# Incoming products of the experts as seven products of halves, outputs summed per 256 hidden columns, and a leaky rectifier in one instruction

## The chip, the cores and the metric

The kernel runs on one core of a Trainium2 chip. A core has TensorE (PE, matrix products into the PSUM banks), VectorE (DVE), ScalarE (ACT), GpSimd (POOL) and SyncE (SP, which issues the transfers). The metric is the device time of one execution in microseconds (us), the median of several.

## The reference

Three steps follow one another. An mLSTM over 2 x 8 heads, 768 positions and head size 40 gives x with 1536 tokens x 320. A dense layer makes g = max(0.01 h, h) with h = x @ w_in (320 x 2048, in 64-bit floats here) and x2 = g @ w_out. Then a mixture of 8 experts, all of them computed for all tokens:

```python
logits = x @ w_gate; logits = logits - logits.max(); P = np.exp(logits)
for _ in range(8):
    P /= P.sum(1, keepdims=True) + 1e-09
    P /= P.sum(0, keepdims=True) + 1e-09
    P *= N / E
for e in range(E):                        # E = 8, w1[e] 320 x 1024, w2[e] 1024 x 320
    h = np.maximum(x @ w1[e], 0.0)
    out += P[:, e:e + 1] * (h @ w2[e])
```

## The kernel before

Every wide product is made of fp32r products: an operand is split into a rounded part ("hi", written by ACT) and the rest ("lo", a subtraction on DVE or POOL), and hi\*hi, hi\*lo and lo\*hi are added up in PSUM. A depth of 320 rows is three row blocks, the third with 64 rows; its hi and lo share one block, so `mm1` (L144) needs eight matmuls for one output tile. `mm2` (L151) is the second layer: three matmuls of 320 columns for 128 tokens and 128 hidden columns.

The first stage (to about 299 us) does the gates, the attention by chunks of 128 positions (`Chunk`) and the dense layer in 96 steps of 128 hidden columns x 256 tokens (`up` L408, `down` L421). In a step ACT makes 0.01 h (L413), DVE the maximum (L414), ACT its hi part (L417), POOL its lo part (L418). Between the steps DVE unpacks the 64-bit weights (L124 to L132). `turn2` transposes the finished x2 into `x2T` (three blocks of 512 tokens) and splits it. This stage is put in order by a planner, by the order of the program and by when it thinks things are ready; the lists `before[g]` and `after[g]` give the order.

The expert stage is in the order in which it is written (`manual_schedule`, L571): each engine takes its instructions strictly one after the other. A group g is one expert, 512 tokens and 128 hidden columns: `up_c` (L651) issues eight matmuls of 512 columns into one PSUM bank, ACT takes hi of the rectified bank (L657), DVE lo (L658); `down_c` (L662), two groups behind, adds 4 x 3 matmuls of 320 columns into four banks `yc`, which are kept for the eight groups of an expert's 1024 columns and only then weighted into `acc` on DVE (L676; for expert 0 copied, L674). There are 8 x 3 x 8 = 192 groups. Beside them: the weights of the next expert, loaded by SP and split on ACT and POOL (L136, L137), and in the first 16 groups or so the gate: `logits`, its transposes, and eight rounds of `rows` (L627, four small DVE instructions) and `columns` (L633, a matmul and four DVE instructions). When the gate is done POOL scales the first expert's outputs (L683).

Of the kernel before, what the change touches and what calls it, by code (L numbers as in the profile page):

```python
# [37 lines left out]
def mlstm_moe_kernel(ctx, tc, qp, q3, kp, kn, vn, gates_in, og, cst_in, scr_in, w_in, w_out, w_gate, w1, w2, out):  # L38
# [23 lines left out]
    xp = ctx.enter_context(tc.tile_pool(name="xp", bufs=2))  # L62
# [23 lines left out]
    class Unit:  # L86


        def __init__(self, w1_ap, w2_ap, nm, is64=False):
            self.src, self.nm, self.is64 = (w1_ap, w2_ap), nm, is64  # L90
            self.t, self.raw, self.up = [None, None], [None, None], [None, None]
# [64 lines left out]

    def transpose_x(ps_pool, x, dst, nm):
# [14 lines left out]
    unitsE = {}  # L172
    x2T, xs2 = {}, {}

    def turn2(j, pool, part=None):
        jb = j * BA // NTC
        if jb not in x2T:
            x2T[jb] = x2p.tile([P, 5, NTC], F32R, tag=f"x2T{jb}", name=f"x2T{jb}")
        for t in (0, 1) if part is None else (part,):
            tok = j * BA + t * P  # L180
            transpose_x(pool, xs2[j][t], x2T[jb][:, :, tok % NTC:tok % NTC + P], f"b{j}_{t}")

    with ExitStack() as st1:
        ac = st1.enter_context(tc.tile_pool(name="ac", bufs=1))
        ap = st1.enter_context(tc.tile_pool(name="ap", bufs=1))
        ha = st1.enter_context(tc.tile_pool(name="ha", bufs=5))
# [81 lines left out]
        kw = ap.tile([P, 9, D], F32, tag="kw", name="kw")  # L268
# [4 lines left out]
        class Chunk:  # L273
# [58 lines left out]
            def weigh(self):  # L332
                self.Pm = self.place([P, 8, P], "Pm", "w1u")
# [38 lines left out]
            def carry(self):  # L372
# [7 lines left out]
                else:  # L380
                    dm = ap.tile([P, G, GV], F32, tag="dm", name=f"dm_{self.nm}")
# [15 lines left out]
        unitsA = [Unit(w_in[i], w_out[i], f"a{i}", wide) for i in range(NUA)]  # L397
        unitsE[0] = [Unit(w1[0, i], w2[0, i], f"e0_{i}") for i in range(NUE)]
# [9 lines left out]
        def up(g):  # L408
# [4 lines left out]
            nc.scalar.activation(gg, h_ps, AF.Copy, scale=0.01)  # L413
            nc.vector.tensor_tensor(gg, h_ps, gg, op=ALU.max)  # L414
# [6 lines left out]
        def down(g):  # L421
# [9 lines left out]
            if f == NFA - 1:  # L431
                xs2[j] = []
                for t in range(2):
                    y = yp[j][t]
                    xs = xp.tile([P, DM], F32, tag="xs", name=f"xs2_{j}_{t}")
# [4 lines left out]
                    xs2[j].append(xs)  # L440
# [27 lines left out]
        before[NFA + HALF + LAG + 0].insert(0, lambda: turn2(1, ps_b))  # L468
        for j in [0] + list(range(2, NBA - 1)):
            before[max(j + 1, 2) * NFA + LAG + 1].insert(0, lambda j=j: turn2(j, ps_b))  # L470
# [28 lines left out]
        for n in range(2 * NUE):  # L499
            i, p = n // 2, n % 2  # L500
            after[g5 - 3 + n].append(lambda i=i, p=p: unitsE[0][i].load(p))
            after[g5 + LAG + 7 + p].append(lambda i=i, p=p: run(unitsE[0][i].convert(p, nc.vector)))
# [16 lines left out]
        zero = ap.tile([P, G * GV], F32, tag="dm", name="zero").bitcast(BF16)  # L519
# [52 lines left out]
    hc = ctx.enter_context(tc.tile_pool(name="hc", bufs=4))  # L572
    cp = ctx.enter_context(tc.tile_pool(name="cp", bufs=1))
    ps_s = ctx.enter_context(tc.tile_pool(name="ps_s", bufs=1, space=PSUM))
    ps_y2 = ctx.enter_context(tc.tile_pool(name="ps_y2", bufs=1, space=PSUM))

    ones = cp.tile([P, P], F32, tag="ones", name="ones")
    nc.gpsimd.memset(ones, 1.0)
    acc = [cp.tile([P, DM], F32, tag=f"acc{t}", name=f"acc{t}") for t in range(NCK)]
    Pg = cp.tile([P, NCK, E], F32, tag="Pg", name="Pg")  # L580

    wgr = cp.tile([P, 3, E], F32, tag="wgr", name="wgr")
    nc.sync.dma_start(wgr, w_gate)
    wg = cp.tile([P, 3, 2, E], F32R, tag="wg", name="wg")
# [240 lines left out]
```

## Time and profile before

| | us |
|---|---|
| Three runs | 1000.46, 1000.84, 1002.84 (median 1000.84) |
| Profiled execution, its own time | 1002.96 |
| Its span | 1001.2 |
| PE busy in the span | 977.7 (98%) |
| DVE, ACT, POOL busy | 378.2, 302.6, 241.6 |
| First and last matmul start of `hc` (expert stage) | 298.9 and 991.9 |

The span is the time from the first to the last instruction; the execution's own time is a little longer. A busy PE is a PE that has work, not one that works at its peak: matmuls overlap in the records, so their pace is read from the distance of their starts. The granted clock of TensorE is given in tenths or as a share: 1.00 is 2.4 GHz, 0.50 is 1.2 GHz.

### The profile page before, as it was taken

To read this page: it belongs to the slowest core of one execution; us is meant where nothing else is said; L and a number is where in the kernel's file an instruction comes from. 1 tells how busy PE (TensorE), PEld (TensorE's weight loads), DVE (VectorE), ACT (ScalarE), POOL (GpSimd) and SP (SyncE) were. 2 spreads that over 40 slices of the span, in tenths; PEclk is the share of its full clock that TensorE was granted. 3 is DMA by queue.
4 is the path that set the end of the run, shared out by engine and by line. 5 is a ranking of instruction groups with operands and counts; after the bars stand their busy time and mean duration, and the time that the engine had idled before them with its cause. 6 is when DMAs were issued, how large, how long until landed. Compare 5 with 4: busy or idle time off the path is not lost.

```text
span 1001.2 us, 14301 instructions
## 1 busy us (share of the span) xinstructions
PE 977.7 (98%) x5917; PEld 886.3 (89%) x5917; DVE 378.2 (38%) x745; ACT 302.6 (30%) x570; POOL 241.6 (24%) x211
## 2 busy tenths in 40 slices
PE   8599999999999999999999999999999999999998
PEld 4488899999998889999999999999999999999997
DVE  5969945343442365222222221222222222222222
ACT  4636444534552221222122122212212212221111
POOL 3454644443430120621012021102202201210000
PEclk8569999999999999999999999999999999999999
DMA  8533503111030110011011011001201100100000
GB/s 264 190 133 108 166 23 105 29 51 38 15 101 16 45 43 16 29 47 42 1 58 44 16 29 59 29 14 45 59 1 43 45 29 14 59 1 1 27 27 27
DMA packets 23526, 52.25 MB, mean 52 GB/s; under 512 B 2614, under 2 KB 9958, under 8 KB 23462
## 3 DMA queue, kind: packets, MB, share of 16 engines
q1 hardware_dynamic: 23462, 51.35, 16.6%
q8 instruction: 46, 0.75, 0.3%
q14 instruction: 18, 0.15, 0.0%
HBM read 49.37 MB, written 1.97 MB: 51 GB/s over the span
## 4 chain that ended last, share of the span: by engine, by line
PE 90%; DVE 6%; DMA 2%; issue 1%; ACT 1%; POOL 1%; SPq 0%; DVEq 0%; POOLq 0%; ACTq 0%
PE hc L146 35%; PE yc L153 11%; PE yc L155 11%; PE yc L154 11%; PE ha L146 8%; PE ya L153 2%; PE ya L154 2%; PE ya L155 2%; PE yps L343 2%; DMA raw_a<-in_w_in_dram 1%; PE sps L329 1%; DVE raw_a L128 1%; PE zps L347 1%; DVE raw_a L132 1%; PE aps L319 1%
## 5 line engine op out<-in xcount | busy, mean ns | idle before, releaser
L146 PE MATMUL hc<-x2T,w1u_e 128*128 128x512 f32 x1536 | 384.0, 392 | 0.0
L146 PEld LDWEIGHTS hc<-x2T,w1u_e 128*128 128x128 f32 x1536 | 280.6, 188 | 49.6
L658 DVE SCALAR_TENSOR_TENSOR hl<-hc,hh 128x512 fp32r<-128x512 f32 x192 | 132.8, 692 | 496.5 <-ACT hh L657 496.5
L657 ACT ACTIVATE hh<-hc 128x512 fp32r<-128x512 f32 x192 | 115.0, 599 | 535.0 <-PE hc L146 531.7
L153 PE MATMUL yc<-w2u_e,hh 128*128 128x320 f32 x768 | 237.5, 309 | 0.6 <-DVE acc L674 0.6
L155 PE MATMUL yc<-w2u_e,hl 128*128 128x320 f32 x768 | 237.3, 309 | 0.0
L154 PE MATMUL yc<-w2u_e,hh 128*128 128x320 f32 x768 | 237.0, 309 | 0.0
L153 PEld LDWEIGHTS yc<-w2u_e,hh 128*128 128x128 f32 x768 | 144.2, 188 | 8.3 <-issue 1.0
L154 PEld LDWEIGHTS yc<-w2u_e,hh 128*128 128x128 f32 x768 | 144.2, 188 | 6.9
L155 PEld LDWEIGHTS yc<-w2u_e,hl 128*128 128x128 f32 x768 | 144.2, 188 | 0.0
L137 POOL TENSOR_TENSOR w1u_e<-raw_e,w1u_e 128x768 fp32r<-128x768 f32 x28 | 51.7, 1847 | 315.5 <-ACT w1u_e L136 315.5
L146 PE MATMUL ha<-xT,w1u_a 128*128 128x256 f32 x768 | 113.3, 292 | 9.8 <-DVE xT L167 3.3
L146 PEld LDWEIGHTS ha<-xT,w1u_a 128*128 128x128 f32 x768 | 104.1, 196 | 15.7 <-ACT xT L165 4.0
L418 POOL TENSOR_TENSOR hla<-gg,hha 128x256 fp32r<-128x256 f32 x90 | 73.9, 822 | 110.4 <-ACT hha L417 93.4
L137 POOL TENSOR_TENSOR w2u_e<-raw_e,w2u_e 128x640 fp32r<-128x640 f32 x28 | 43.9, 1568 | 145.9 <-ACT w2u_e L136 145.9
L414 DVE TENSOR_TENSOR gg<-ha,gg 128x256 f32<-128x256 f32 x96 | 40.3, 421 | 69.4 <-ACT gg L413 69.1
L153 PE MATMUL ya<-w2u_a,hha 128*128 128x320 f32 x192 | 62.8, 327 | 0.0
L154 PE MATMUL ya<-w2u_a,hha 128*128 128x320 f32 x192 | 60.8, 317 | 0.0
L155 PE MATMUL ya<-w2u_a,hla 128*128 128x320 f32 x192 | 60.7, 316 | 0.0
L413 ACT ACTIVATE gg<-ha 128x256 f32<-128x256 f32 x96 | 36.7, 382 | 73.2 <-PE ha L146 73.2
L417 ACT ACTIVATE hha<-gg 128x256 fp32r<-128x256 f32 x96 | 39.9, 416 | 46.0 <-DVE gg L414 45.8
L676 DVE SCALAR_TENSOR_TENSOR acc<-yc,Pg,acc 128x320 f32<-128x320 f32 x84 | 40.3, 543 | 2.6 <-PE yc L155 2.6
(138 smaller groups left out, 695.7 us busy)
## 6 DMA issues: line engine op xcount, KB each, us to landing
raw_e<-in_w_dram SPq DMA_DIRECT2D x32, 384.0 KB, 3.1
raw_e<-in_w_dram SPq DMA_DIRECT2D x32, 320.0 KB, 2.9
raw_a<-in_w_in_dram SPq DMA_DIRECT2D x8, 768.0 KB, 5.2
raw_a<-in_w_out_dram SPq DMA_DIRECT2D x8, 640.0 KB, 3.9
kP_c<-in_kp_dram SPq DMA_DIRECT2D x11, 256.0 KB, 3.1
qP_c<-in_qp_dram SPq DMA_DIRECT2D x11, 256.0 KB, 3.8
vt_c<-in_vn_dram SPq DMA_DIRECT2D x11, 184.5 KB, 2.5
sig<-in_og_dram SPq DMA_DIRECT2D x3, 640.0 KB, 7.3
```

The costliest lines, as they stand in the source:

```text
L137: (lo or nc.gpsimd).tensor_tensor(t[:, n:2 * n], src, t[:, 0:n].bitcast(F32), op=ALU.subtract)
L146: nc.tensor.matmul(h_ps, t1[:, ws, c * P:(c + 1) * P], xt[:, xs, t0:t0 + n], start=(j == 0), stop=(j == len(MM1) - 1),)
L153: nc.tensor.matmul(y_ps, a, t2[:, c, :], start=first, stop=False)
L154: nc.tensor.matmul(y_ps, a, t2[:, 2 + c, :], start=False, stop=False)
L155: nc.tensor.matmul(y_ps, b, t2[:, c, :], start=False, stop=last)
L413: nc.scalar.activation(gg, h_ps, AF.Copy, scale=0.01)
L414: nc.vector.tensor_tensor(gg, h_ps, gg, op=ALU.max)
L417: nc.scalar.activation(hh, gg, AF.Copy)
L418: (nc.vector if g in V_STEPS else nc.gpsimd).tensor_tensor(hl, gg, hh.bitcast(F32), op=ALU.subtract)
L657: nc.scalar.activation(hh, h_ps, AF.Relu)
L658: nc.vector.scalar_tensor_tensor(out=hl, in0=h_ps, scalar=0.0, in1=hh.bitcast(F32), op0=ALU.max, op1=ALU.subtract)
L676: nc.vector.scalar_tensor_tensor(out=acc[tt], in0=yc[t], scalar=Pg[:, tt, e:e + 1], in1=acc[tt], op0=ALU.mult, op1=ALU.add)
```

## The change

**Expert stage.** The work is now cut into 32 units of 256 hidden columns (`Products`, four to an expert) times two halves of 768 tokens: 64 steps. Depth (2 x 160), hidden columns (2 x 128) and tokens (2 x 384) are each halved, and the 2 x 2 x 2 product is made with seven products in place of eight: each takes a sum or difference of weight blocks (`sums`) and one of token blocks (`Position.sums`). A half depth of 160 is a block of 128 rows and one of 32; of the latter the three terms (hi, lo) lie in one block of 96 rows. So one product is three matmuls with 128 rows and one with 96, all of 384 columns: 28 per step. Partial products stay in four banks; DVE adds them up from PSUM and SBUF (`u2`, `u3` and three `c`), ACT rectifies each `c` twice (rounded and full), POOL takes the difference; the fourth output is still made as before. `down_c` now ends after 256 hidden columns: six token blocks, 2 x 3 matmuls each, through three rotating banks, and each is added to `acc` on DVE: six DVE instructions per step. `Position` turns and splits x2: three positions of the first half at the end of the first stage, three of the second half in the first steps of the expert stage. Work beside the matmuls is hung at slots (step, slot): slots 0 to 6 follow the seven products of the next step, 7 to 12 the six token blocks.

**First stage.** One ACT instruction with the function Prelu replaces the scaled copy and the maximum. `turn2` is gone. The small tiles of the attention lie as views in the room that later holds the split x2.

**Gate.** The logits read the new blocks (30 matmuls of 384 columns in place of 15 of 512); a round is spread over seven slots.

```diff
-            nc.scalar.activation(gg, h_ps, AF.Copy, scale=0.01)
-            nc.vector.tensor_tensor(gg, h_ps, gg, op=ALU.max)
+            nc.scalar.activation(gg, h_ps, AF.Prelu, alpha=0.01)
...
+        def load1(self):                          # class Products
+            for h in range(2):
+                nc.sync.dma_start(dst[:, h, :, 0], src[:, h])
+                for r in range(4):
+                    nc.sync.dma_start(dst[r * KM:(r + 1) * KM, h, :, 1], src[h * KM:(h + 1) * KM, 2])
+        def sums(self, eng, part=None):
+            for k, (o, x, y, op) in enumerate(((4, 1, 3, ALU.add), (1, 0, 1, ALU.subtract), (5, 4, 0, ALU.subtract),
+                                               (6, 2, 5, ALU.subtract))):
+                if part is None or k in part:
+                    eng.tensor_tensor(r[:, o], r[:, x], r[:, y], op=op)
+        def split1(self, k, lo, rest):
+            split7(self.raw[:, (0, 4)[k]:(4, 7)[k]], self.w1[k], slice(0, P), KM, lo, rest)
+        def split2(self, lo):
+            nc.scalar.activation(t[:, 0:2], self.raw2, AF.Copy)
+            lo.tensor_tensor(t[:, 2:4], self.raw2, t[:, 0:2].bitcast(F32), op=ALU.subtract)
+    def split7(raw, dst, t, r0, lo, rest):
+        nc.scalar.activation(dst[:, :, 0:2, t], raw.rearrange("p n (s t) -> p n s t", s=2), AF.Copy)
+        lo.tensor_tensor(dst[:, :, 2, t], raw[:, :, 0:P], dst[:, :, 0, t].bitcast(F32), op=ALU.subtract)
+        r = slice(r0, r0 + KM)
+        rest.tensor_tensor(dst[r, :, 1, t], raw[r, :, P:2 * P], dst[r, :, 1, t].bitcast(F32), op=ALU.subtract)
+        def turn(self, k, pool, copy):            # class Position, k = 0 or 1
+            if k == 0:
+                for i, x in enumerate((xa, xb)):
+                    copy(self.rr[:, i]..., x[:, 2 * P:DM]...)
+            for j, (i, x, h) in enumerate(((0, xa, 0), (0, xa, 1), (1, xb, 1), (1, xb, 0))):
+                nc.tensor.transpose(pt[:, j, :], self.rr[:, i, h] if k else x[:, h * P:(h + 1) * P], ident)
+            nc.scalar.activation(self.raw[:, 0:4, k * P:(k + 1) * P], pt, AF.Copy)
+        def sums(self, eng):
+            for o, x, y in ((5, 2, 3), (3, 3, 0), (4, 2, 3), (6, 1, 4)):
+                eng.tensor_tensor(r[:, o], r[:, x], r[:, y], op=ALU.subtract)
...
+        for g, fn in ((g5 - 6, experts[0].load1), (g5 + 1, lambda: prepare_position(positions[0][0])),
+                      (g5 + 5, lambda: prepare_expert(experts[0])), (g5 + 6, experts[0].load2),
+                      (g5 + 6, lambda: prepare_position(positions[0][1])), (g5 + 7, experts[1].load1),
+                      (g5 + 10, lambda: prepare_position(positions[0][2])),
+                      (g5 + 11, lambda: experts[0].split2(nc.gpsimd)), (g5 + 11, experts[1].load2),
+                      (g5 + 13, lambda: prepare_expert(experts[1])), (g5 + 14, experts[2].load1)):
+            after[g].append(fn)
...
+    def product(bank, u, q, w, x, fresh):
+        f, b = u.factor(w), X[q][:, x]
+        nc.tensor.matmul(bank, f[:, 0], b[:, 0], start=fresh, stop=False, skip_group_check=not fresh)
+        nc.tensor.matmul(bank, f[:, 0], b[:, 2], start=False, stop=False, skip_group_check=not fresh)
+        nc.tensor.matmul(bank, f[:, 2], b[:, 0], start=False, stop=False, skip_group_check=not fresh)
+        nc.tensor.matmul(bank, f[0:K3, 1], b[0:K3, 1], start=False, stop=True, skip_group_check=not fresh)
+    def up_c(i):
+        def out_of(a, b, part, plus):
+            nc.vector.tensor_tensor(c, part, plus, op=ALU.add)
+            nc.scalar.activation(hh[a][b], c, AF.Relu)
+            nc.scalar.activation(c, c, AF.Relu)
+            nc.gpsimd.tensor_tensor(hl[a][b], c, hh[a][b].bitcast(F32), op=ALU.subtract)
+        product(bank[0], u, q, 0, 0, True)
+        nc.scalar.activation(p1, bank[0], AF.Copy)
+        product(bank[1], u, q, 5, 4, True)
+        nc.vector.tensor_tensor(u2, bank[1], p1, op=ALU.add)
+        product(bank[2], u, q, 1, 5, True)
+        nc.vector.tensor_tensor(u3, bank[2], u2, op=ALU.add)
+        product(bank[3], u, q, 4, 3, True)
+        out_of(1, 1, bank[3], u3)
+        product(bank[0], u, q, 2, 1, False)
+        nc.scalar.activation(hh[0][0], bank[0], AF.Relu)
+        nc.vector.scalar_tensor_tensor(out=hl[0][0], in0=bank[0], scalar=0.0, in1=hh[0][0].bitcast(F32), ...)
+        product(bank[2], u, q, 3, 6, False)
+        out_of(1, 0, bank[2], u2)
+        product(bank[3], u, q, 6, 2, False)
+        out_of(0, 1, bank[3], u2)
...
+    for p, (t0, t1, g, s) in enumerate((((-1, 0), (-1, 3), -1, 5), ((-1, 6), (0, 2), 0, 3), ((0, 5), (0, 8), 0, 9))):
+        hook(*t0, turn_x1(p, 0))
+        hook(*t1, turn_x1(p, 1))
+        hook(g, s, lambda p=p: fill_x1(p))        # sums on DVE, split on ACT, DVE and POOL
+    at0, PERIOD = 2 * 13 + 7, 7                   # rows and columns: a round every 7 slots
+            hook(7 + q, (0, 0, 1, 1, 2, 2)[t], lambda q=q, t=t: scale_first(q, t))
+    hook(-1, 2, lambda: experts[2].sums(nc.vector))
+    for n in range(3, NU):
+        u, g = experts[n], max(2 * n - 4, 3)
+        hook(g - 2, 0, u.load1)
+        for k in range(4):
+            hook(g, 8 + k, lambda u=u, k=k: u.sums(nc.gpsimd, (k,)))
+        hook(g + 1, 8, lambda u=u: u.split1(0, nc.gpsimd, nc.gpsimd))
+        hook(g + 1, 10, lambda u=u: u.split1(1, nc.gpsimd, nc.gpsimd))
+        hook(g + 1, 12, u.load2)
+        hook(g + 2, 8, lambda u=u: u.split2(nc.gpsimd))
```

## Rows read from the trace of the kernel before

**Rows 1.** Stages: stretch, its length, PE, PEld, DVE, ACT, POOL busy (instructions), clock, DMA.

```profile
70.00:125.00 55.00, 51.49 (x389) 47.27 (x389) 51.51 (x100) 29.84 (x66) 28.70 (x25) 1.00 0.44 139
125.00:268.00 143.00, 142.89 (x1142) 137.88 (x1141) 62.93 (x165) 63.95 (x150) 59.62 (x76) 1.00 0.15 43
268.00:298.80 30.80, 30.48 (x232) 30.21 (x232) 14.69 (x29) 18.60 (x44) 13.44 (x17) 1.00 0.26 75
298.80:405.00 106.20, 105.61 (x594) 93.05 (x594) 46.46 (x113) 25.84 (x44) 15.80 (x10) 1.00 0.11 34
405.00:997.70 592.70, 592.59 (x3303) 537.26 (x3302) 151.63 (x249) 130.86 (x212) 92.61 (x58) 1.00 0.10 30
```

**Rows 2.** Timeline of one group of the expert stage: start, length, instructions.

```profile
602.24 2.00 PE L146 MATMUL hc<-x2T,w1u_e 128*128 128x512 f32 x8
604.08 0.30 PE L153 MATMUL yc<-w2u_e,hh 128*128 128x320 f32 x1
...
605.83 2.00 PE L146 MATMUL hc<-x2T,w1u_e 128*128 128x512 f32 x8
```

**Rows 3.** Groups of instructions, whole span: count, busy us, mean ns, idle before.

```profile
L658 DVE SCALAR_TENSOR_TENSOR hl<-hc,hh 128x512 fp32r<-128x512 f32 x192 | 132.8, 692 | 496.5 <-ACT hh L657 496.5
L676 DVE SCALAR_TENSOR_TENSOR acc<-yc,Pg,acc 128x320 f32<-128x320 f32 x84 | 40.3, 543 | 2.6 <-PE yc L155 2.6
L414 DVE TENSOR_TENSOR gg<-ha,gg 128x256 f32<-128x256 f32 x96 | 40.3, 421 | 69.4 <-ACT gg L413 69.1
L417 ACT ACTIVATE hha<-gg 128x256 fp32r<-128x256 f32 x96 | 39.9, 416 | 46.0 <-DVE gg L414 45.8
L137 POOL TENSOR_TENSOR w1u_e<-raw_e,w1u_e 128x768 fp32r<-128x768 f32 x28 | 51.7, 1847 | 315.5 <-ACT w1u_e L136 315.5
L137 POOL TENSOR_TENSOR w2u_e<-raw_e,w2u_e 128x640 fp32r<-128x640 f32 x28 | 43.9, 1568 | 145.9 <-ACT w2u_e L136 145.9
```

**Rows 4.** The same view, shapes kept apart.

```profile
L136 ACT ACTIVATE w1u_e<-raw_e 128x768 fp32r<-128x768 f32 x32 | 26.8, 838 | 0.9 <-DMA raw_e<-in_w_dram 0.9
L683 POOL TENSOR_SCALAR acc<-acc,Pg 128x320 f32<-128x320 f32 x12 | 12.8, 1087 | 27.0 <-DVE Pg L631 24.2 <-DVE Pg L639 2.8
L137 DVE TENSOR_TENSOR w1u_e<-raw_e,w1u_e 128x768 fp32r<-128x768 f32 x4 | 3.8, 959 | 3.2 <-ACT w1u_e L136 3.2
L211 ACT ACT_TABLE_LOAD x2 | 2.6, 1283 | 0.0
```

**Rows 5.** Timeline of DVE and POOL in two stretches of the expert stage.

```profile
351.40 0.25 DVE L636 TENSOR_REDUCE cs<-cps 128x8 f32<-128x96 f32 x1
351.68 1.76 DVE L637 TENSOR_SCALAR cs<-cs 128x8 f32<-128x8 f32 x1
353.72 0.26 DVE L639 SCALAR_TENSOR_TENSOR Pg<-Pg,cs 128x96 f32<-128x96 f32 x1
382.10 0.17 DVE L637 TENSOR_SCALAR cs<-cs 128x8 f32<-128x8 f32 x1
...
351.57 1.85 POOL L137 TENSOR_TENSOR w1u_e<-raw_e,w1u_e 128x768 fp32r<-128x768 f32 x1 [5.09 <-ACT w1u_e L136]
...
598.50 1.85 POOL L137 TENSOR_TENSOR w1u_e<-raw_e,w1u_e 128x768 fp32r<-128x768 f32 x1 [5.73 <-ACT w1u_e L136]
599.70 0.55 DVE L676 SCALAR_TENSOR_TENSOR acc<-yc,Pg,acc 128x320 f32<-128x320 f32 x1
```

**Rows 6.** Timeline of PE around matmuls with fewer than 128 rows, and a transpose.

```profile
236.03 0.27 PE L164 MATMUL pt_b<-cst,xs 128*64 128x128 f32 x1
236.14 0.38 PE L162 MATMUL pt_b<-cst,xs 128*128 128x128 f32 x2
...
239.14 0.31 PE L155 MATMUL ya<-w2u_a,hla 128*128 128x320 f32 x1
239.38 0.72 PE L319 MATMUL aps<-bd,stt 32*128 32x512 f32 x2
240.04 1.22 PE L146 MATMUL ha<-xT,w1u_a 128*128 128x256 f32 x8
...
242.80 0.91 PE L347 MATMUL zps<-Cst,q 120*128 120x123 f32 x6
```

More of the change, by code (lines that the diff above doesn't have):

```diff
@@ L171, in mlstm_moe_kernel @@
     NBA = NT // BA
[L172 to L181, printed above, removed]
+    x2s, X = {}, {}
+    R0 = x2p.tile([P, 21 * NQ], F32, tag="R0", name="R0")
+    experts = [Products(w1[e, i], w2[e, i], f"e{e}_{i}") for e in range(E) for i in range(NUE)]
+    positions = [[Position(q, p) for p in range(HP)] for q in range(2)]
     with ExitStack() as st1:
@@ L396, in mlstm_moe_kernel @@
         NG = NBA * NFA
-        unitsA = [Unit(w_in[i], w_out[i], f"a{i}", wide) for i in range(NUA)]
-        unitsE[0] = [Unit(w1[0, i], w2[0, i], f"e0_{i}") for i in range(NUE)]
+        unitsA = [Unit(i, w_in[i], w_out[i], f"a{i}", wide) for i in range(NUA)]
         chunks = [Chunk(c) for c in range(NCK)]
@@ new lines, in mlstm_moe_kernel, with down_c @@
+    ny = [0]
+    def down_c(i):
+        n, q = order[i]
+        u = experts[n]
+        e = n // NUE
+        hh, hl = hidden.pop(i)
+        if q not in acc:
+            acc[q] = x2p.tile([P, 2 * HP, DM], F32, tag="XT", name="acc1")
+        for b in range(2):
+            for p in range(HP):
+                t = b * HP + p
+                k = ny[0] % 3
+                ny[0] += 1
+                y = (ps_y, ps_y, ps_y2)[k].tile([P, DM], F32, tag=("ya0", "ya1", "yb0")[k], name=f"y{i}_{t}")
+                for a in range(2):
+                    mm2(y, hh[a][b], hl[a][b], p, u.w2, a, a == 0, a == 1)
+                o = acc[q][:, t]
+                if n == 0:
+                    nc.vector.tensor_copy(o, y)
+                elif e == 0:
+                    nc.vector.tensor_tensor(o, y, o, op=ALU.add)
@@ L682, in scale_first @@
-    def scale_first(t):
-        nc.gpsimd.tensor_scalar(out=acc[t], in0=acc[t], scalar1=Pg[:, t, 0:1], scalar2=None, op0=ALU.mult)
-    before = {g: [] for g in range(NGC + LAGC)}
-    after = {g: [] for g in range(NGC + LAGC)}
-    for i in range(2):
-        before[(1, 3)[i]].append(lambda i=i: turn2(NBA - 1, ps_s, i))
-    for j in range(NB):
-        before[(5, 4, 8)[j]].append(lambda j=j: logits(j))
-    G0 = 9
-    before[G0].append(logits_turn)
-    before[G0 + 1].append(top_turn)
-    before[G0 + 2].append(top_all)
@@ L695, in mlstm_moe_kernel @@
-    for it in range(8):
-        after[G0 + 2 + 2 * it].append(rows)
-        before[G0 + 4 + 2 * it].append(lambda it=it: columns(it))
-    for t in range(NCK):
-        after[NS + LAGC + t // 2].append(lambda t=t: scale_first(t))
-    for e in range(1, E):
-        for n in range(2 * NUE):
-            i, p = n // 2, n % 2
-            g = (e - 1) * NS + LAGC + 2 * n
-            after[g].append(lambda e=e, i=i, p=p: units[e][i].load(p))
-            after[g + 3].append(lambda e=e, i=i, p=p: run(units[e][i].convert(p)))
@@ L706, in mlstm_moe_kernel, with scale_first, copy_rest @@
-    for g in range(NGC + LAGC):
-        if g < NGC:
-            up_c(g)
-        for fn in before[g]:
-            fn()
-        if g >= LAGC:
-            down_c(g - LAGC)
-        for fn in after[g]:
-            fn()
+                    nc.sync.dma_start(out[row:row + P, :], o)
+                at(i, 7 + t)
+    def scale_first(q, t):
+        o = acc[q][:, t]
+        nc.gpsimd.tensor_scalar(out=o, in0=o, scalar1=Pg[:, 2 * HP * q + t, 0:1], scalar2=None, op0=ALU.mult)
+    def copy_rest(o, i):
+        nc.gpsimd.tensor_copy(o, i)
@@ L718 @@
+    up_c(0)
+    for i in range(len(order)):
+        if i + 1 < len(order):
+            up_c(i + 1)
+        down_c(i)
+    assert not hooks
 _OUTS = [((1536, 320), 'float32')]
```

247 lines of the change are left out of this document (164 added, 83 removed).

## Prediction

> **What bounds the kernel now.** I read the busy time by stage first [rows 1]. The expert stage takes 298.8 to 997.7, 698.9 us; PE is busy for all of it, DVE for a quarter of 405 to 997.7 and POOL for a sixth. From 125 to 298.8 PE is the bound too. Only 70 to 125 has another: DVE 51.5 of 55 us. The timeline gives PE's pace [rows 2]: a group begins at 602.24, its 320-column matmuls at 604.08, the next group at 605.83. So a 512-column matmul costs 1.84/8 = 0.230 us, a 320-column one 1.75/12 = 0.146, a group 3.59, and 192 groups 689.3 of the 698.9; 9.6 are the gate and transposes. The span of 1001.2 lies 1.8 under the profiled execution's 1002.96, and that lies 2.1 above the median of 1000.84. I work on 1002.96 and take off 2.1 at the end.
>
> **The change, part by part.**
>
> *Matmuls of the experts.* A 384-column matmul lies between the two: 0.146 + 64/192 x 0.084 = 0.174. A step has 28 of them, 4.87 us, and 36 of 320 columns, 5.26: 10.13. The same work is now three groups, 10.77. Saved: 0.64 x 64 = **41.0 us**. In proportion to columns 384 costs 0.1725 to 0.175, so 38 to 44 us. A weight load is hidden already beside 320 columns.
>
> *Matmuls with 96 rows.* A quarter of the 28. The trace has 32 and 120 rows [rows 6]. With 32 rows: 0.24 from the matmul before (0.146 expected), 0.72 - 0.39 = 0.33 from the first to the second of 512 columns (0.230 expected; 0.39 is one's recorded length, 2.00 - 7 x 0.230), 0.33 to the next; some 0.09 lost on entry and 0.09 on exit. With 120 rows six take 0.91, 0.11 to 0.13 apart, what the 128-column transposes take too (236.03 to 236.14): no loss. Bounds 0 and 448 x 0.185 = +83 us; I take 0, since 96 is nearer to 120 and, like it, doesn't fit in half of the rows. The Trainium skill (TensorEngine Tiling, Key Properties) says that a change of the tiling mode drains TensorE, and lists modes of 128, 64 and 32 rows. The 32-row matmuls agree; by that list 96 rows run in the 128-row mode and cost nothing, and the sum would be mine. No run so far shows 96.
>
> *Other PE work.* In the expert stage 30 logits matmuls at 0.174 (5.2) for 15 at 0.230 (3.45), 24 transposes at 0.11 for 8: **+3.5**. In the first stage 40 transposes go and 24 come: **-1.8**.
>
> *A step's other engines.* DVE: six operations of 384 columns, 0.557 each (between 421 ns for 256 and 692 for 512), and six additions into `acc` at 0.543: 6.6 of 10.13. ACT: eight of about 0.5, and of the weights per two steps 1.05 + 0.84 + 0.73: 5.3. POOL costs 2.18 ns a column (1847 to 1568 ns over 128 columns): 0.73 for 256, 1.01 for 384, 1.29 for 512; per two steps 6 x 1.01 + 4 x 0.73 + 2 x 1.29 + 2 x 1.01 + 1.57 = 15.2 of 20.3 [rows 3, 4]. None is over. The tightest wait inside a step: product 3 ends 2.95 us after the step's start (16 x 0.174 and 0.16 by which a record outlasts its pace); DVE's `c` 3.51, two rectifiers of 0.52 4.55, the fourth output's hi on ACT 5.05, its lo on DVE 5.61, two more `c` 6.72, the first `acc` addition 7.27. Its bank is wanted again by the fourth token block at 4.87 + 3 x 0.876 = 7.50. It holds, by 0.23: **0**; bounds 0 and +32 (0.5 a step).
>
> *Filling the second half's blocks* (steps -1 and 0). Each of three `fill_x1` puts on DVE four subtractions (0.42 each) and a low part of 896 columns (959 ns for 768: 1.09), and between them DVE waits for ACT's copy of 1792 columns (0.82 ns a column: 1.7). Behind that waiting subtraction stand the last `c` of the step and the next `u2`, `u3`; product 3 and 5 of the next step wait for their banks, and all PE behind them. So a fill takes DVE 4.5 us, three 13.4, expert 2's `sums` 1.7, the steps' own work (12 x 0.557 and 6 copies) 9.6: 24.7 us where PE has 2 x 4.87 + 5.26 + 2.6 = 17.6. That is 7.1 over. Further, DVE and POOL get in each other's way: an 8-element DVE instruction took 1.76 us and ended with POOL's subtraction, which had begun 0.1 before it; alone it takes 0.17. An `acc` addition, which reads PSUM, took its 0.55 beside POOL [rows 5]. All fill operations are of SBUF alone, 19 of them with `sums`, and POOL has some 22 us of work in this stretch (six low parts 6.1, splits of units 1 and 2 6.2, three rests of 896 columns 6.4, six copies some 3.6): 0.25 each, 5 more. **+12**; bounds 0 (later steps wait less) and +18.
>
> *The gate's rounds* fall on 7 slots of 13, 1.86 rounds a step, over 4.3 steps. A round is two series of DVE instructions of about 1.0 us unhindered (351.40 to 353.98 less the 1.6 waited), so 3.7 a step: with 6.3 it just fits in 10.13. POOL is busy 75% of the time with operations of 1 us, so each of four SBUF instructions in a round waits 0.38: 12 us in eight rounds, part of it in time where DVE would be idle. `columns` stands in PE's queue four slots behind `rows`, so a late DVE stops PE. **+7**; bounds 0 and +20.
>
> *Units 3 and scaling.* Unit 3 is split during `down_c(4)` and wanted directly after it: POOL ends its four subtractions 13.7 us after that step's start, the matmuls want them from 10.6: about 2.5, part of it covered by the waits above. `scale_first` puts 12 x 1.087 us on POOL in two steps where it has 15.2 of 20.3 to do [rows 4]. Together **+3**; bounds 0 and +6.
>
> *First stage.* 21 of the 96 maxima lie in 70 to 125, 21 x 0.42 = 8.8 us of DVE's 51.5. Half of it moves PE: **-4**; bounds -9 and 0. At its end (268 to 298.8) DVE gets three positions (3.9 each) and two experts (2.95 each), 17.5, and loses maxima, x2T and the old splits, 14.8. ACT gets 15.7 and loses 7.3: 27 of 30.8 busy, in bursts of 3.7 us in front of the rectifiers that free two banks. X[0] must be whole before the first product. **+4**; bounds 0 and +12. Prelu itself takes what the scaled copy took. If it isn't in the table that holds Exp, every chunk's Exp adds two loads of 1.283 us [rows 4], 20 of them 26 us of ACT, of which half is idle: 0 to +13; I take 0, since the copies beside Exp load nothing. The Trainium skill (ScalarE: Activation LUTs, Table sets) says that cheap functions lie in every set and names relu, copy, identity and abs; the leaky one is not named. By it the sum would be mine or 13 more; the five loads of the trace agree with it for the named ones.
>
> *Transfers.* Ten for a unit's first weights in place of one, all on SP, issued two steps (20 us) ahead; the DMA engines are 10% busy [rows 1] and nothing but loads and the last outputs stands in that queue. 0.
>
> Sum: -41.0 + 3.5 - 1.8 + 12 + 7 + 3 - 4 + 4 = -17.3; 1002.96 - 17.3 = 985.7, and less 2.1: **983.5 us**.
>
> **The rivals.**
> *Clean start.* The waits of the first steps vanish, because DVE's delays fall into the down phases, where PE needs nothing of it for 5 us: 1000.84 - 41 + 1.7 - 4 = 957.5. For it: four of the terms are overlaps that I added up one by one. Against: three fills stand within 1.5 steps.
> *Narrow matmuls drain PE* (the other side). Each of 448 matmuls of 96 rows costs 0.185 as with 32 rows: 983.5 + 83 - 12 (the waits of the first steps are then covered) = 1055. It decides from 17.3/448 = 0.039 us each. For it: the 32-row rows. Against: the 120-row one.
> *The chain in a step is late.* The 0.23 us of slack are gone and each step waits 0.4: 983.5 + 25.6 = 1009; it decides from 0.27 a step. For it: five hand-overs between ACT and DVE, each some hundredths, are not in my chain. Against: instructions of one engine that follow each other overlap somewhat in the records.
> *The product count doesn't become time*: PE's pace set by weight loads, 28 for 24. Against: 128-column transposes follow at 0.11, under 0.174. Under 1 in 50.
>
> **How the numbers follow.** Forecast 983.5, own range 967 to 999 (the bounds of the first steps' terms): 0.57. Clean start, 950 to 966: 0.17. Chain late, 1000 to 1020: 0.11. Narrow matmuls, 1040 to 1066: 0.07. The rest, 0.08, is Prelu's loads and a first stage put in another order by the planner, 990 to 1010. The range 957 to 1010 leaves out the lower half of the clean start, the narrow matmuls and the late end of the chain, 2 in 10. A change under 0.3% (3 us) can't be told from none. Faster: 0.57 + 0.17 + 0.03 = 0.77; same 0.06; slower 0.17.
>
> **What would show it.** Distance of 384-column matmul starts 0.174, also into and out of 96 rows; a steady step of 10.1 us; waits of PE for DVE in the first 60 us of the expert stage that add up to about 20, and next to none later; the first `product` at about 297 to 300; no more table loads than five. Wrong would make it: steady steps over 10.4 us, DVE's `acc` additions longer than 0.55, POOL over 16 us per two steps, or first steps without waits.

## The result, and the profile after

The changed kernel takes 1008.11 us (median of five, 1007.07 to 1010.63), the kernel before 1000.82 in the same runs (999.90 to 1002.84): ratio 1.0073, 95% interval 1.0054 to 1.0092. It is **slower**, by 0.7%: little, but the interval lies wholly above 1. The forecast was 983.5. The profiled execution took 1007.07, its span 1005.4.

The stages of the kernel after (columns as in [rows 1]):

```profile
70.00:125.00 55.00, 51.93 (x404) 48.68 (x404) 41.84 (x74) 29.00 (x66) 26.40 (x25) 1.00 0.37 114
125.00:268.00 143.00, 142.01 (x1126) 136.93 (x1124) 37.65 (x97) 64.77 (x151) 61.16 (x76) 1.00 0.15 46
297.90:360.00 62.10, 46.33 (x261) 41.36 (x260) 31.35 (x61) 27.27 (x48) 28.94 (x27) 0.86 0.12 32
360.00:455.00 95.00, 82.84 (x493) 79.96 (x492) 64.87 (x155) 37.40 (x71) 62.42 (x63) 0.96 0.09 26
455.00:1001.70 546.70, 546.70 (x3433) 546.39 (x3432) 336.39 (x643) 266.69 (x501) 395.84 (x393) 1.00 0.15 42
```

The first product comes at 297.90, as forecast. Before, PE worked from 298.8 to the end almost without a gap and at a granted clock of 1.00 [rows 1]. Now only the last row looks so. In the two above it PE lacks 28 us of work, and the clock is 0.86 and 0.96. The timeline of a steady step:

```profile
598.41 0.33 PE L777 MATMUL b<-X,w_e 128*128 128x384 f32 x1
...
600.34 0.34 PE L780 MATMUL b<-X,w_e 96*128 96x384 f32 x1
600.51 0.34 PE L777 MATMUL b<-X,w_e 128*128 128x384 f32 x1
...
603.34 0.31 PE L157 MATMUL y<-w_e,hh 128*128 128x320 f32 x1
...
608.62 0.34 PE L777 MATMUL b<-X,w_e 128*128 128x384 f32 x1
```

The step begins at 598.41 and its down phase at 603.34, so 28 matmuls of 384 columns take about 4.9 us and 36 of 320 take 5.28; steps from 455 on take 10.20 us in the mean. Three groups took 10.77 [rows 2]. Into and out of a 96-row matmul the starts are 0.17 to 0.18 apart, as between two of 128 rows. Groups of the kernel after, shapes kept apart:

```profile
L848 DVE SCALAR_TENSOR_TENSOR acc<-y,Pg,acc 128x320 f32<-128x320 f32 x336 | 179.1, 547 | 63.7 <-PE y L159 57.6
L796 DVE TENSOR_TENSOR c<-b,s 128x384 f32<-128x384 f32 x192 | 100.4, 550 | 15.6 <-PE b L780 8.2 <-POOL w_e L205 4.1 <-POOL hl L799 2.4
L232 DVE TENSOR_TENSOR rawx<-rawx 128x256 f32<-128x256 f32 x24 | 16.9, 703 | 4.6 <-ACT rawx L226 4.0
L207 POOL TENSOR_TENSOR X<-rawx,X 32x896 fp32r<-32x896 f32 x3 | 8.8, 2930 | 10.4 <-ACT X L204 10.4
L411 ACT ACT_TABLE_LOAD x2 | 2.6, 1283 | 0.0
```

The additions are as long as assumed (543 and 557). The subtractions of the fills are not: 703 against 421 [rows 3] (675 for the twelve of the second half). There are five table loads (two of them in the last row), as before. What PE waited for from 298 to 455 (us in total, times, longest):

```profile
PE px L225 <- POOL rr L861: 6.4, 1, 6.4
PE px L225 <- ACT w_e L204: 6.0, 1, 6.0
PE y L157 <- DVE acc L846: 5.1, 3, 3.4
PE b L777 <- DVE c L796: 3.6, 3, 1.6
PE b L777 <- DVE s L808: 2.6, 2, 1.5
PE y L157 <- DVE acc L844: 2.4, 1, 2.4
PE cps L747 <- DVE Pg L743: 1.0, 1, 1.0
PE px L225 <- ACT rawx L226: 0.7, 1, 0.7
```

27.8 us in 13 waits: px is the turning of the second half, y the down phases, cps the rounds, b the products. How the 6.0 arises, followed through DVE, ACT, POOL and PE:

```profile
308.99 2.56 DVE L232 TENSOR_TENSOR rawx<-rawx 128x256 f32<-128x256 f32 x4
311.58 1.70 ACT L204 ACTIVATE X<-rawx 128x1792 fp32r<-128x1792 f32 x1 [1.40 <-DVE rawx L232]
313.31 1.09 DVE L205 TENSOR_TENSOR X<-rawx,X 128x896 fp32r<-128x896 f32 x1 [1.76 <-ACT X L204]
313.42 2.92 POOL L207 TENSOR_TENSOR X<-rawx,X 32x896 fp32r<-32x896 f32 x1 [2.15 <-ACT X L204]
314.32 0.55 DVE L796 TENSOR_TENSOR c<-b,s 128x384 f32<-128x384 f32 x1
315.46 0.52 ACT L798 ACTIVATE c<-c 128x384 f32<-128x384 f32 x1
316.42 1.01 POOL L799 TENSOR_TENSOR hl<-c,hh 128x384 fp32r<-128x384 f32 x1
317.36 0.75 POOL L861 COPY rr<-x 128x256 f32<-128x256 f32 x2
317.82 1.11 PE L225 MATMUL px<-cst,rr 128*128 128x128 f32 x4 [5.98 <-ACT w_e L204]
```

The first four rows are fill 0. The last `c` of step 0 stands behind it on DVE, its rectifiers behind that on ACT, `hl` behind those on POOL, the copies of `rr` behind `hl`, and PE's transposes behind `rr`. (POOL has its own part of the fill in front of `hl` too: the rectifier ended at 315.98, that part at 316.34.) So a transpose for the *next* fill, whose blocks are first read at 352.6, stops all matmuls for 6 us. (The profile names ACT's split of unit 2 as the releaser; what ends just before the transpose starts is the first of the two `rr` copies.)

### The profile page after: what moved, and what is told of

Its sections match the earlier page's. It is cut to its first block, busy times and chain, and to the rows that moved or that the text cites. A ratio compares the mean times of both kernels' runs of the same rounds, so it can differ in the third digit from the quotient of the medians.

```text
span 1005.4 us, 16882 instructions
## 1 busy us (share of the span) xinstructions
PE 948.7 (94%) x6188; PEld 918.3 (91%) x6188; DVE 590.6 (59%) x1146; ACT 479.8 (48%) x935; POOL 631.1 (63%) x629
## 4 chain that ended last, share of the span: by engine, by line
PE 74%; DVE 12%; POOL 4%; issue 4%; ACT 3%; DMA 2%; SPq 1%; DVEq 0%; ACTq 0%; POOLq 0%
PE y L157 10%; PE y L158 10%; PE y L159 10%; PE b L777 7%; PE b L780 7%; PE b L779 7%; PE b L778 7%; PE ha L150 6%; PE ya L157 2%; PE ya L159 2%; PE ya L158 2%; PE yps L434 1%; DVE raw_a L132 1%; DVE rawx L232 1%; POOL acc L858 1%
## 5 line engine op out<-in xcount | busy, mean ns | idle before, releaser
L799 POOL TENSOR_TENSOR hl<-c,hh 128x384 fp32r<-128x384 f32 x192 | 196.0, 1023 | 186.5 <-ACT c L798 145.3
L157 PE MATMUL y<-w_e,hh 128*128 128x320 f32 x768 | 239.3, 312 | 7.4 <-DVE acc L846 5.1
L158 PE MATMUL y<-w_e,hh 128*128 128x320 f32 x768 | 238.4, 310 | 0.0
L159 PE MATMUL y<-w_e,hl 128*128 128x320 f32 x768 | 237.9, 310 | 0.0
L848 DVE SCALAR_TENSOR_TENSOR acc<-y,Pg,acc 128x320 f32<-128x320 f32 x336 | 179.1, 547 | 63.7 <-PE y L159 57.6
L777 PE MATMUL b<-X,w_e 128*128 128x384 f32 x448 | 154.7, 345 | 6.3 <-DVE c L796 3.6
L157 PEld LDWEIGHTS y<-w_e,hh 128*128 128x128 f32 x768 | 145.0, 189 | 9.1 <-DVE acc L846 5.9
L780 PE MATMUL b<-X,w_e 96*128 96x384 f32 x448 | 152.5, 340 | 0.0
L779 PE MATMUL b<-X,w_e 128*128 128x384 f32 x448 | 152.2, 340 | 0.0
L778 PE MATMUL b<-X,w_e 128*128 128x384 f32 x448 | 151.8, 339 | 0.0
L158 PEld LDWEIGHTS y<-w_e,hh 128*128 128x128 f32 x768 | 145.1, 189 | 0.0
L159 PEld LDWEIGHTS y<-w_e,hl 128*128 128x128 f32 x768 | 145.1, 189 | 0.0
L150 PE MATMUL ha<-xT,w_a 128*128 128x256 f32 x768 | 112.7, 289 | 10.4 <-ACT gg L503 3.7
L150 PEld LDWEIGHTS ha<-xT,w_a 128*128 128x128 f32 x768 | 102.8, 194 | 16.3 <-ACT gg L503 5.2
L777 PEld LDWEIGHTS b<-X,w_e 128*128 128x128 f32 x448 | 85.9, 192 | 8.5 <-DVE c L796 4.6
L778 PEld LDWEIGHTS b<-X,w_e 128*128 128x128 f32 x448 | 86.1, 192 | 0.0
```

The lines of the kernel that those rows point to most:

```text
L150: nc.tensor.matmul(h_ps, t1[:, ws, c * P:(c + 1) * P], xt[:, xs, t0:t0 + n], start=(j == 0), stop=(j == len(MM1) - 1),)
L157: nc.tensor.matmul(y_ps, a, t2[:, c, :], start=first, stop=False)
L158: nc.tensor.matmul(y_ps, a, t2[:, 2 + c, :], start=False, stop=False)
L159: nc.tensor.matmul(y_ps, b, t2[:, c, :], start=False, stop=last)
L777: nc.tensor.matmul(bank, f[:, 0], b[:, 0], start=fresh, stop=False, skip_group_check=not fresh)
L778: nc.tensor.matmul(bank, f[:, 0], b[:, 2], start=False, stop=False, skip_group_check=not fresh)
```

## The experiments

The first stage is the same code in most of these kernels, yet the first product came between 297.9 and 303.6 in it, with a mean clock of 0.66 to 0.80 in the first 70 us. So beside the times I give the **expert stage** of the profiled execution: end of the span less the start of the first product. It is 702.3 us before and 707.5 after. The same stage came to 707.2 and 708.2 in e9 and e10, so differences of about 1 us say nothing.

**e1: no fills.**

```diff
-    X[1] = cp.tile([P, 7, 3, NQ], F32R, tag="X1", name="X1")
+    X[1] = X[0]                    # and the nine hooks of turn_x1, fill_x1 are gone
```

> Leaves out the turning and filling of the second half's three positions; the second half's products read the blocks of the first half instead. Theory (the fills make PE wait, through DVE and ACT waiting for each other, and PE's clock falls after these waits): the two waits of 6 us for px go, the falls of the clock at 307 to 335 with them; 2.3 us of transposes, some 15 us of waits and some 5 us of cold matmuls: 983 to 988 us, steps -1 to 2 at 11 us each. Rival (the first steps are slow because of the late gate weights, the splits of unit 2 and cold matmuls, whatever is filled): only the transposes and a few us go, 1000 to 1005 us.

989.89 us, just above the theory's range; ratio to before 0.989 [0.983, 0.995]; expert stage 688.1, 19.4 less. The slots of -1 and 0 (the products of steps 0 and 1 and the first down phase) take 21.4 us in place of 40.0; later steps change little. So the fills cost 17.3 us beside their 2.1 us of transposes (six times 0.357).

**e2: no rounds.**

```diff
-    hook(2, 7, rows)
-    for it in range(8): ...        # columns, columns_end, rows
```

> Leaves out the eight rounds that normalise rows and columns (the gate is only the exponential). Theory (the rounds' small DVE instructions, behind POOL's and in front of the acc additions, make PE wait): 1.3 us of matmuls, some 12 us of waits in 355 to 440 and the two falls of the clock at 379 and 396 (3.4) go: 990 to 993 us, steps of 5.0 and 5.3 us there. Rival (POOL is late with the weights of units 3 and 4 in these steps, rounds or not): 1003 to 1006 us, and PE still waits there.

998.11, between the two; ratio 0.996 [0.994, 0.999]; expert stage 697.3, 10.2 less. The steps of the rounds come down to 10.2 us, but step 6, the first with unit 3, takes 12.1 us for its products (4.9 steady). PE's waits from 355 to 455:

```profile
PE b L779 <- POOL w_e L205: 1.8, 1, 1.8
PE b L780 <- POOL w_e L207: 1.5, 2, 0.9
PE b L777 <- DVE c L796: 1.3, 1, 1.3
```

The waits at y are gone. Both were partly right: POOL's split of unit 3 is late, and in the changed kernel, where no wait for it shows, the rounds' waits covered it.

**e3: gate weights loaded early.**

```diff
+        wgr = const.tile(...); nc.gpsimd.memset(wgr, 0.0); nc.sync.dma_start(wgr[...], w_gate[...])   # first stage
```

> The gate weights are cleared and loaded at the start of the first stage; nothing else moves. Theory (DVE stands 7.6 us for them until 302.4, and the first u2, u3 behind it): the first down-phase starts 3 us earlier, 1004 to 1006 us. Rival (the wait is hidden: the first fill's sums and ACT set the pace of these steps anyway): 1007 to 1009 us, the wait for px grows by what is saved.

1011.31, above both; ratio 1.012 [1.006, 1.018]; expert stage 705.9, 1.6 less, hardly more than such stages differ by themselves; the px wait grew from 5.98 to 7.45. The 7.6 us for which DVE had stood were mostly covered by the fill. The profiled execution is longer because the first product came at 303.6. Six transfers more in SP's queue at the start may be why, or the spread of that stage (e7, whose first stage is unchanged, had 303.6 too); neither was tried by itself.

**e4: fills hung apart**, gate and scaling a step later.

```diff
-        positions[1][p].sums(...); positions[1][p].split(...)      # one slot: (-1,5), (0,3), (0,9)
+    sums (0,6) (0,11) (1,7)   ACT's split (0,7) (1,0) (1,8)   low parts (0,9) (1,3) (1,10)
```

> The same instructions of the fills on the same engines, but hung apart: the four subtractions, ACT's split and the low parts each two slots later than what they wait for, most in the down phases of steps 0 and 1 and between the first products of step 2; the second half's logits, the rounds and the scaling a step later. Theory A (queues in strict order: DVE and ACT wait for each other in a fill, with the c's behind them): the two 6 us waits and their cold matmuls shrink, 993 to 999 us. Rival B (what costs is that DVE and POOL work on SBUF at the same time): the same work beside the same work, 1005 to 1010 us, with the DVE sums still at a mean of 700 ns.

1005.39, ratio 1.004 [1.001, 1.007]; expert stage 704.0. The slots of -1 and 0 took 29.0 in place of 40.0, but some five of the 11 us came back in the next two steps (the down phase of step 1 took 9.7 for 7.1), where the last fill met POOL's work (its sums took 1.1 us each in the mean); the mean of all twelve sums rose from 675 to 875 ns. Five more went to step 6, where unit 3 is late again (12.2 us of products for 7.3). A was right on where the waits came from, B on the time and on a part of what replaced them.

**e5: all of it placed anew**, on the same engines. Hooks, as 13 x step + slot:

```
              after                        e5                           e8
sums          -8, 3, 9                     0, 11, 16                    7, 9, 16
ACT's split   the same slots               10, 13, 23                   10, 12, 17
low parts     the same slots               12, 19, 23                   13, 18, 21
columns       37, 44, 51 ... 86            42, 49, 54, 61, 67, 79 ...   43, 47, 53, 62, 71, 80 ...
unit 3        sums 47-50, splits 60, 62    28-36, 40, 53                29-35, 38, 44
gate weights  start of the expert stage    end of the first stage       as e5
```

> Same instructions on the same engines as the changed kernel, all fills, rounds and units kept; only their places among the steps of the expert stage are others (gate weights loaded late in the first stage; rr copies ahead of the low parts; the sums, ACT's split and the low parts of a fill five to ten slots apart; DVE's small instructions of the rounds where POOL has little to do; unit 3 and 4 split steps earlier). Theory (PE's 28 us of waits in 298 to 455 come from DVE, ACT and POOL waiting for each other in strict order, and from DVE and POOL holding each other up on SBUF; 13 us of cold matmuls follow from these waits): all but some 8 us go, the expert stage takes 672 to 682 in place of 707.5, the execution 970 to 983 us, clock 1.0 nearly throughout. Rival (the first 150 us have too much work for DVE and POOL wherever it stands): waits return at other places, 995 to 1006 us.

992.07, ratio 0.990 [0.987, 0.993]: faster than before, and between what theory and rival expected. Expert stage 689.5, 18 less than after, short of the 672 to 682 expected: PE still waited 6.3 us at five `columns` and 5.0 in two waits for `u3`.

**e6: rounds without POOL.**

```diff
+            hook(g + 1, 10, lambda u=u, n=n: setattr(u, "w1", experts[n - 3].w1))     # units 3, 4: no sums, no split
+            if 2 <= i <= 9: nc.scalar.activation(hl[a][b], c, AF.Copy)               # in place of POOL's subtraction
```

> As the changed kernel, but POOL has next to nothing to do in steps 2 to 5, where the rounds stand: the splits of units 3 and 4 are left out (their matmuls read the blocks of units 0 and 1), and in steps 2 to 9 the low part of the three c is a plain copy on ACT. Fills and rounds are unchanged. Theory B (the rounds cost time because their small DVE instructions wait until POOL's instruction ends): PE's waits between 355 and 445 fall from 12 us to under 4, the small instructions keep to 0.17 to 0.27 us each, 994 to 998 us. Rival A (the chain of a round, DVE, PE, DVE, is too long for its seven slots by itself): waits of 9 us or more stay, 1003 to 1008 us.

1004.34, a time of A's range; ratio 1.003 [1.000, 1.006]; expert stage 704.0. The small instructions by line, kernel after first (ns: min/median/max), then e6 (us, mean ns):

```profile
L740 DVE TENSOR_REDUCE rs<-Pg x8: 252/253/254, 362.4 to 416.8; 128x12 f32<-128x96 f32 x8
L742 DVE RECIPROCAL rs<-rs x8: 227/228/229, 363.2 to 417.3; 128x12 f32<-128x12 f32 x8
L741 DVE TENSOR_SCALAR rs<-rs x8: 172/358/1145, 362.7 to 417.1; 128x12 f32<-128x12 f32 x8
L743 DVE TENSOR_TENSOR Pg<-Pg,rs x8: 257/362/1119, 363.5 to 417.6; 128x96 f32<-128x96 f32 x8
L753 DVE SCALAR_TENSOR_TENSOR Pg<-Pg,cs x8: 257/552/1336, 367.6 to 422.8; 128x96 f32<-128x96 f32 x8
```

```profile
L741 DVE TENSOR_SCALAR rs<-rs 128x12 f32<-128x12 f32 x8 | 1.4, 173 | 0.3
L743 DVE TENSOR_TENSOR Pg<-Pg,rs 128x96 f32<-128x96 f32 x8 | 2.1, 258 | 0.3
L753 DVE SCALAR_TENSOR_TENSOR Pg<-Pg,cs 128x96 f32<-128x96 f32 x8 | 2.1, 258 | 0.3
```

With POOL idle these three never stretch; beside it they take up to 6.7 times as long, while the reduction and the reciprocal keep their length. The Trainium skill (SBUF — State Buffer, Who interferes with whom) says that DVE and GpSimd share a port pair under an exclusive lock, which a DVE instruction with two SBUF inputs, or one of the copy and tensor-scalar kind, can take, and that a reduction does not contend. The trace agrees with that; the reciprocal isn't named there. But PE's waits from 355 to 445 fell only from 10.5 to 6.6 us. 2.4 of these follow the exponential, which stands on ACT behind the added copies, and a new wait of 1.8 us for ACT at 351.9 came with the copies too. So both theories hold a part: POOL's meeting with the rounds is worth some 4 to 6 us of waits, and 4 of the 10.5 stay without it.

**e7: no rounds, unit 3 a step earlier.**

```diff
-            hook(g, 8 + k, lambda u=u, k=k: u.sums(nc.gpsimd, (k,)))
+            hook(g - (n == 3), 8 + k, lambda u=u, k=k: u.sums(nc.gpsimd, (k,)))       # the splits likewise
```

> The eight rounds are left out as before, and POOL forms and splits unit 3 one step earlier. Theory (without rounds the step that first uses unit 3 took 12.1 us in place of 4.9, because POOL ends unit 3's blocks only then; with rounds their waits hid it): that step takes 5 us, the expert stage 690 in place of 697, 989 to 993 us. Rival (POOL has too much to do there at any place): the wait moves to another step, 996 to 1000 us.

992.90, ratio 0.991 [0.988, 0.994]; expert stage 689.7, as expected, and the products of step 6 take 4.9. So the rounds and the late unit 3 together cost 17.8 us, 1.2 of them matmuls: 10.2 went with the rounds (e2), 7.6 more with unit 3. No run has the rounds with unit 3 alone moved, so how the 17.8 divide stays open.

**e8: placed once more** (third column of the table; rounds where POOL has little to do, scaling from slot 99 on).

> As the placed version (same instructions, same engines as the changed kernel), with the places chosen once more from what its trace shows: there PE still waits 7 us for the rounds' Pg (five waits of 0.9 to 1.7 us at the columns matmuls), 2.2 us in step 2 and 2.9 us at the scaling. Now each columns matmul stands later behind its rows, units 3 and 4 are split before most rounds, the scaling ends a step earlier. Theory (order and meeting of DVE and POOL): about 10 of the 16 us of waits and 5 of the 10 us of cold matmuls go, the expert stage takes 674 to 682 in place of 689.5, 976 to 986 us. Rival (the rest is work, not place): 988 to 993 us.

982.69, ratio 0.981 [0.978, 0.984]: the fastest of all. Expert stage 681.7. Its waits from 298 to 455, and two stretches:

```profile
PE cps L749 <- DVE Pg L745: 2.9, 4, 0.9
PE y L157 <- DVE acc L846: 1.8, 1, 1.8
PE y L157 <- DVE acc L848: 1.4, 2, 1.3
PE y L157 <- DVE acc L850: 1.3, 2, 0.8
...
```

```profile
298.00:360.00 62.00, 57.33 (x348) 52.31 (x348) 44.19 (x88) 34.63 (x62) 41.61 (x43) 0.97 0.10 28
360.00:455.00 95.00, 90.99 (x564) 88.89 (x564) 63.02 (x156) 41.50 (x78) 70.97 (x70) 1.00 0.13 37
```

8.6 us of waits in place of 27.8, and with them went the low clock: 0.97 and 1.00 for 0.86 and 0.96. The fill's subtractions still meet POOL, and are longer than in the changed kernel (822 ns for 675), but nothing that PE wants soon stands behind them.

**e9: the changed kernel again**, on the chip that ran e8.

> The changed kernel itself, unchanged, so that the placed versions are compared with it on one chip: 1004 to 1010 us, expert stage 706 to 709 us.

1010.53, ratio to before 1.008 [1.005, 1.011], expert stage 707.2: slower again, by half a microsecond more than expected at most. So e8 is 27.8 us (2.8%) below it, 25.5 of them in the expert stage.

**e10: without Prelu.**

```diff
-            nc.scalar.activation(gg, h_ps, AF.Prelu, alpha=0.01)
+            nc.scalar.activation(gg, h_ps, AF.Copy, scale=0.01)
+            nc.vector.tensor_tensor(gg, h_ps, gg, op=ALU.max)
```

> The changed kernel with the scaled copy and the maximum of before in the first stage's 96 steps in place of Prelu. Theory (the prediction's step: 21 maxima of 0.42 us fall into 70 to 125, where DVE is busy most, and half of that moves PE): DVE's busy time there rises from 42 to about 50 us, the first product comes 3 to 6 us later than in the unchanged kernel of the same job. Rival (DVE no longer bounds that stretch, so the maxima are hidden): the first product comes within 2 us of it.

1014.16, ratio 1.011 [1.006, 1.016]; expert stage 708.2. DVE is busy 51.3 us of 70 to 125 (40.6 in e9). The first product comes at 304.0, 5.4 later than in e9; but e2 and e4, whose clock in the first 125 us was like e10's (0.66, then 0.97), had it at 301.3 and 301.7. At like clock Prelu is worth about 2.5 us, and the medians less the expert stages (1014.16 to 1010.53, 708.2 to 707.2) say 2.6. But e6 and e7, both at 0.76 over the first 70 us, differ by 3.8 in the first product, so the size isn't firmly shown.

**e11: fills without POOL.**

```diff
-    hook(0, 0, lambda: experts[2].split1(0, nc.gpsimd, nc.gpsimd)); hook(0, 1, ...)
+    hook(0, 0, lambda: setattr(experts[2], "w1", experts[0].w1))     # no rests in the fills; hl of steps 0 to 2 a copy on ACT
```

> As the changed kernel, with POOL nearly empty while the fills run: the rest of each fill (the subtraction of 32 rows x 896) and unit 2's sums and splits on POOL are left out (its matmuls read unit 0's blocks), and in steps 0 to 2 the low part of the three c is a plain copy on ACT; only the copies of rr and one split of second weights stay on POOL. DVE's and ACT's part of the fills stands where it stood. Theory A (DVE and ACT wait for each other in strict order, and the transposes stand behind both): the waits before px stay at 8 to 11 of 12.4 us, steps -1 to 0 take 34 to 38 of 40 us, 1001 to 1005. Theory B (DVE is held up by POOL on SBUF): the waits fall under 4 us, the sums of a fill take 1.5 us in place of 2.6 to 4.1, 992 to 998.

1007.79, ratio 1.006 [1.003, 1.009]; expert stage 705.9. The fill's subtractions, and PE's longest waits from 298 to 345:

```profile
L232 DVE TENSOR_TENSOR rawx<-rawx 128x256 f32<-128x256 f32 x12 | 5.1, 422 | 0.3
```

```profile
PE px L225 <- ACT rawx L226: 8.4, 3, 3.8
PE b L777 <- DVE s L811: 1.8, 1, 1.8
```

The subtractions are back at 422 ns, but 8.4 of 13.1 us before px stay, now with ACT's copy of px named: A, though the time lies above its 1001 to 1005. The slots of -1 and 0 took 36.6 us. So POOL's part of the fills is worth some 5 us of these waits. (The added copies lengthen ACT's queue, so order's own part may be somewhat less than 8.4.)

**e12: engines moved too**: two rests and unit 4's sums on DVE, the scaling on ACT.

```diff
-        nc.gpsimd.tensor_scalar(out=o, in0=o, scalar1=Pg[...], scalar2=None, op0=ALU.mult)
+        nc.scalar.activation(o, o, AF.Copy, scale=Pg[...])
```

> As the second placed version, but with instructions moved to engines that have room: two of the three rests of a fill and unit 4's sums on DVE, the scaling of the first expert's outputs on ACT (0.5 us in place of POOL's 1.09). Theory (what is left of waits comes from POOL's queue and from meeting it on SBUF): 4 us less than the second placed version, 977 to 981. Rival (DVE becomes the engine that is late): 982 to 988.

990.96, ratio 0.990 [0.986, 0.994]; expert stage 688.5, 6.8 more than e8. PE waits 4.5 us for `acc` at y and 3.4 at `columns`: DVE is late, as the rival said, though the time lies above its 982 to 988 too. Its slots differ from e8's, so this isn't the engines alone.

## Why the prediction was wrong

Much of what it said held: PE's pace, losses in the first steps (though 12 of the 28 us of waits came after the first 60 us, where it had next to none), no late chain in the steady step, no cost of 96 rows. The Trainium skill's rule on tiling modes (TensorEngine Tiling, Key Properties) was read rightly for 96 rows: no drain shows in the starts, 0.17 to 0.18 us apart. The direction was wrong because the losses of the first steps, which the sum put at 22 us, were 37.5. Term by term, expert stage first:

| step | forecast | measured | from |
|---|---|---|---|
| matmuls | -41.0 | -36.5 | steady step 10.20, not 10.13 |
| logits, transposes | +3.5 | +3.4 | transposes 2.1 for 0.7, logits 5.3 for 3.4, columns |
| fills | +12 (0 to 18) | +17.3 | e1: 19.4 less 2.1 |
| rounds, with the late unit 3 | +7 (0 to 20) | +16.6 | e7: 17.8 less 1.2 |
| unit 3, scaling | +3 (0 to 6) | +2, scaling alone | one step at the scaling 12.2 |
| gate weights | not named | +1.6 | e3 |
| expert stage | -15.5 | +5.2 | 702.3 to 707.5 |
| Prelu | -4 (-9 to 0) | about -2.5 | e10 |
| first product | -1.8 | -1.0 | 298.9 to 297.9 |

The measured rows of the stage add up to 4.4; 0.8 is open. Each loss lies within its own bounds, but both large ones near the upper end, and the range of 967 to 999 didn't allow for that. That the first product came within 1 us of the forecast is luck: the spread of that stage is 5.7. None of the four signs of being wrong that the prediction named came (steps of 10.20, additions of 547 ns, POOL at 14.8 us per two steps, waits in the first steps): they didn't test the terms that failed. Three causes:

*The fills and the rounds were added up as loads.* The step that failed reads "a fill takes DVE 4.5 us ... 7.1 over" and "3.7 a step: with 6.3 it just fits in 10.13". A load that fits says nothing about what stands behind it. In both places an instruction that is wanted late stands in front of one that PE wants at once, through up to four queues. So PE waited elsewhere than the prediction said: beside the fills only 2.6 us at the products for their banks, but 13.1 us at the transposes, which the sum charged with 0.11 each and no wait; and for the rounds 1.0 at `columns`, but 7.5 at the token blocks (y), whose additions into `acc` stand behind the small instructions on DVE. Without rounds these 7.5 are gone (e2). The same instructions on the same engines, in other places, give 25.5 us back (e8 against e9; the earlier gate weights among them).

*POOL.* I had seen the 1.76 us beside POOL [rows 5] and charged 0.25 to 0.38 per instruction. In the trace the three stretched lines of a round that are shown above cost 0.30, 0.28 and 0.36 us more in the mean (476, 542 and 618 ns beside POOL), the fourth (L751) 0.15, and a subtraction of the fills 0.25 (675 for 421), so the price was about right; that they stand in PE's way each time was not in it.

*The clock.* The sum took 2.4 GHz throughout. After its waits PE ran at 1.2 GHz in five stretches, 24 us in all; two of them in the kernel after:

```profile
307.30:310.70 3.40, 3.01 (x11) 3.01 (x12) 2.55 (x6) 1.76 (x4) 1.45 (x2) 0.50 0.00 0
314.10:321.00 6.90, 3.18 (x12) 3.13 (x13) 2.58 (x6) 4.29 (x8) 6.66 (x7) 0.51 0.18 49
```

```profile
319.37 0.52 PE L779 MATMUL b<-X,w_e 128*128 128x384 f32 x1
319.69 0.52 PE L780 MATMUL b<-X,w_e 96*128 96x384 f32 x1
```

The first follows waits of 1.5, 1.1 and 0.7 us that ended at 304.0, 306.0 and 307.7, the second holds the 6.0 us wait for px. PE was busy 16.3 of the 24 us. Its starts there lie 0.32 us apart for 384 columns and 0.267 for 320, in place of 0.1757 and 0.147, so some 45% of that, 7 us, is loss. Unhindered, 64 steps of 10.20 with logits, transposes and the rounds' matmuls (9.8) and an end of 3.8 would be 666.4 us; of the 41.1 above it 27.8 are waits and 7 the clock (an estimate). 6 are left: a wait counts only from the end of the last record, 0.16 us after its pace, which makes 2 us in 13 waits, and the rest stays open.

And a small one: 0.07 us in a step (0.1757 us in the mean in place of the interpolated 0.174, 0.1468 in place of 0.146) became 4.5 us over 64 steps.

The rival "clean start" (957.5) set the waits to nothing, and no run came there: e8, at 681.7, is still 15.3 above 666.4. That e8's time equals the forecast is chance: its terms are others.

## What to carry to other kernels

Where engines run strictly in order, price an inserted piece of work by what stands *behind* it on its engine and on every engine that waits for that, not by whether the load fits; split it at each hand-over and hang the parts so that the other engine has finished before the waiting one arrives. Splitting by itself isn't enough: e4 won 3.5 us, e8 25.5. Put what is wanted late behind what is wanted now, on PE's queue too: a transpose for later stops all matmuls. A change that speeds the steady state can lose all of it in its first steps (here 157 of 707 us), and the profile's waits by stage show this at once.

## What the runs showed of the hardware that I had not expected

- The granted clock of the same first stage varied from run to run (0.66 to 0.80 over the first 70 us), and the first product by up to 5.7 us. The two don't go strictly together: at 0.76 it came at 299.8 (e6) and 303.6 (e7), at 0.66 at 301.3 (e2). Changes of 0.3% need the stage's own length, not the total.
- POOL waits for DVE as DVE for POOL: the 32 x 896 subtraction took 2.93 us in the mean where it began 0.1 us after DVE's low part of 1.09 us; where it didn't begin behind one it took 2.11 to 2.16 (e4, e5).
- Prelu over 256 columns takes ACT 0.38 us, and no table load is added beside Exp.
